# A spectral filter and a two-layer network on one core: the first batch's stages reordered and its last one regrouped, the second batch's first stage split between two engines

## The chip, the cores and the metric

One core of one Trainium2 chip. In the profiles PE is the tensor engine (matmuls), PEld its weight loads, DVE the vector engine, ACT the scalar engine and POOL (Pool) GpSimd; PSUM is the memory that matmuls write to, and a cast here is a copy out of it to 16 bits. The granted clock is the share of its full clock that PE was given. The metric is the device time of one execution in microseconds. Each kernel is run several times. Before: 793.71 us median of 6 runs (792.79 to 795.1).

## The reference

`x` is (8, 3008, 256). Each batch is filtered along its 3008 positions in the frequency domain, and the result goes through a leaky two-layer network.

```python
X = np.fft.rfft(x, axis=1)
Y = X * (filt_r + 1j * filt_i)[None]
y = np.fft.irfft(Y, n=3008, axis=1)          # (8, 3008, 256)
h = y.reshape(24064, 256) @ w_in             # 256 -> 2048
out = np.maximum(0.01 * h, h) @ w_out        # 2048 -> 256, float32
```

## The kernel before

The transform is split as 3008 = 94 x 32. Per batch: stage 1 (`s1`, 94-point matmuls), a transpose on DVE (`t1`), stage 2 and the filter (`s2`, DVE and Pool multiply), the inverse of stage 2 (`sa`), a second transpose (`t2`) and the last stage (`sb`), which leaves `yts`, columns by token. Then PE runs the network in 47 chunks of 512 tokens with 8 slots each. The first batch runs alone, because nothing dense can start before it is done; the other batches are strewn over the slots by `plan`.

```python
def s1_group(b, g):                    # 2 matmuls, then one cast PSUM -> SBUF on ACT
    ...
    spread(big[(4 * b) % 3], 2 * g, ps, nc.scalar.copy)

def spread(dst, n0, ps, copy, e0=0):   # column d goes to pair e = d // 2, place t = d % 2
    copy(paired(dst)[:, ds(n0, nn), ds(e0, de)], ps[:].rearrange("p n (e t) -> p n e t", t=2))

def t2_part(b, i):                     # 32 x 32 transposes of pairs seen as 4-byte words
    a = big[(4*b+2) % 3]...            # read in order e, n
    o = big[(4*b+3) % 3]...rearrange("p (h n e) -> p h e n", h=2, n=Q)
    nc.vector.transpose(o[:, i // 2, ts(i % 2, E4), :], a)     # one word, then 256 bytes on

def sb_group(b, g, copy, pool=(pfp, "pf")):
    for j in range(4):
        nc.tensor.matmul(ps[:, j, :], src[:, dt, 4 * h + j, :], i1_sb[:, 4 * h + j, :], ...)
    copy(yv[:, :, ds(4 * h, 4)], ps[:].rearrange("p c a -> p a c"))
...
# the first batch, in halves of 128 columns; True: Pool multiplies (ACT brings it the PSUM), False: DVE
upper(0)
first_s2(0, 0, 8, False)
first_s2(0, 8, 8, True)
first_s2(0, 16, 4, False)
first_s2(0, 20, 4, True)
for g in range(8): first_s1(1, g, ...)
t1_part(0, 2, True)(), t1_part(0, 3, True)()
first_sa(0, 0), first_sa(0, 16)
upper(1)                               # 2.75 us of ACT and 0.95 of DVE: filter rows copied
first_s2(1, 0, 8, False)
first_s2(1, 8, 8, True)
first_sa(0, 8), first_sa(0, 20)
first_s2(1, 16, 8, False)
first_sa(1, 0)
t2_part(0, 0)(), t2_part(0, 1)()
first_sa(1, 16), first_sa(1, 8)
t2_part(0, 2)(), t2_part(0, 3)()
keep_warm(5)                           # 5 matmuls whose result nobody reads
...                                    # sb_group 0 to 7
keep_warm(3)
...                                    # sb_group 8 to 15
plan(1, 0, 0, 3, 6, 10, 4, 3, 25, 31)  # batch 1: s1 from slot 0, t1 slot 6, s2 slot 10, t2 25, sb 31
```

Pool's products go to a pool of four buffers shared with the output tiles (`outp.tile([P, n, DH], FP16, tag="ost")`); each `first_s2(..., True)` takes two of them.

Of the kernel before, what the change touches and what calls it, by code (L numbers as in the profile page):

```python
# [10 lines left out]
P = 128  # L11
FP16 = mybir.dt.float16
FP32 = mybir.dt.float32
# [5 lines left out]
N1, N2 = 94, 32  # L19
NC = 24  # L20
Q = 32
# [44 lines left out]
def kernel(  # L66
# [9 lines left out]
    nc = tc.nc  # L76
# [18 lines left out]
    i1_sb = cpool.tile([P, N2, N1], FP16, name="i1_sb")  # L95
# [6 lines left out]
    big = [cpool.tile([P, Q * D], FP16, name=f"big{i}") for i in range(3)]  # L102
    yts = [cpool.tile([P, NDT, N], FP16, name=f"yt{i}") for i in range(2)]
# [16 lines left out]
    DH = D // 2  # L120

    def x_load(b, n0=0, nn=N2, d0=0, dn=D):

        for lo, cnt in ((0, R1),) if b + 1 < B else ((0, 64), (64, N1 - 64)):
            nc.gpsimd.dma_start(  # L125
                x_sb[lo : lo + cnt, ds(n0, nn), ds(d0, dn)],
                bass.AP(tensor=x.tensor, offset=x.offset + (b * N + lo * N2 + n0) * D + d0,
                        ap=[[N2 * D, cnt], [D, nn], [1, dn]]))
# [10 lines left out]
    step = N2 // FP  # L139
# [15 lines left out]
    nc.vector.memset(big[2][:].rearrange("p (e n t) -> p e n t", n=Q, t=2)[:, :, NC:Q, :], 0.0)  # L155


    def s1_group(b, g):
        def go():
            ps = pfp.tile([P, 2, D], FP32, tag="pf", name=f"s1_b{b}_g{g}")  # L160
            for j in range(2):
                n2 = 2 * g + j
                nc.tensor.matmul(ps[:, j, :], f1_sb[:N1, n2, :], x_sb[:N1, n2, :],  # L163
                                 start=True, stop=True)
            spread(big[(4 * b) % 3], 2 * g, ps, nc.scalar.copy)
        return go


    def paired(t):
        return t[:].rearrange("p (e n t) -> p n e t", n=Q, t=2)  # L170

    def spread(dst, n0, ps, copy, e0=0):
        nn, de = ps.shape[1], ps.shape[2] // 2
        copy(paired(dst)[:, ds(n0, nn), ds(e0, de)], ps[:].rearrange("p n (e t) -> p n e t", t=2))  # L174

    E4 = D // 2 // 4

    def t1_part(b, i, flat=False):
        def go():
            a = big[(4 * b) % 3][:].bitcast(FP32)[:, ts(i, E4 * Q)].rearrange("p (e n) -> p e n", n=Q)  # L180
            o = big[(4 * b + 1) % 3][:].bitcast(FP32)
            if flat:
                o = o[:, ts(i, E4 * Q)].rearrange("p (e n) -> p e n", n=Q)
            else:
                o = o.rearrange("p (n e) -> p e n", n=Q)[:, ts(i, E4), :]
            nc.vector.transpose(o, a)  # L186
        return go


    def t2_part(b, i):  # L190
        def go():
            a = big[(4 * b + 2) % 3][:].bitcast(FP32)[:, ts(i, E4 * Q)].rearrange("p (e n) -> p e n", n=Q)
            o = big[(4 * b + 3) % 3][:].bitcast(FP32).rearrange("p (h n e) -> p h e n", h=2, n=Q)
            nc.vector.transpose(o[:, i // 2, ts(i % 2, E4), :], a)  # L194
        return go
# [19 lines left out]
    def sa_group(b, g):  # L215
        def go():
            ps = pfp.tile([P, 2, D], FP32, tag="pf", name=f"sa_b{b}_g{g}")
            nc.tensor.matmul(ps[:], inv2, ys.pop((b, g))[:], start=True, stop=True)  # L218
            spread(big[(4 * b + 2) % 3], 2 * g, ps, nc.scalar.copy)
        return go  # L220

    def sb_group(b, g, copy, pool=(pfp, "pf")):
        dt, h = g // 8, g % 8

        def go():
            src = big[(4 * b + 3) % 3][:].rearrange("p (h n d) -> p h n d", h=2, n=Q)
            ps = pool[0].tile([P, 4, N1], FP32, tag=pool[1], name=f"sb_b{b}_g{g}")
            for j in range(4):
                n2 = 4 * h + j
                nc.tensor.matmul(ps[:, j, :], src[:, dt, n2, :], i1_sb[:, n2, :],  # L230
                                 start=True, stop=True)
            yv = yts[b % 2][:, dt, :].rearrange("p (a c) -> p a c", c=N2)
            copy(yv[:, :, ds(4 * h, 4)], ps[:].rearrange("p c a -> p a c"))  # L233
        return go


    two = ((pfp, "pf"), (php, "ph"))
    act, dve = nc.scalar.copy, nc.vector.tensor_copy
# [10 lines left out]
    def first_s2(hf, c, n, on_pool):  # L249
        ps = php.tile([P, n, DH], FP32, tag="ph", name=f"f2_h{hf}_c{c}")  # L250
        src = paired(big[1])
        for j in range(0, n, 4):
            nc.tensor.matmul(ps[:, ds(j, 4), :].rearrange("p n (e t) -> p n e t", t=2), fwd2,  # L253
                             src[:, ds(c + j, 4), ts(hf, DH // 2)], start=True, stop=True)
        fs = [f[:, ds(c, n), ts(hf, DH)] for f in (fa_sb, fb_sb)]
        if on_pool:
            y = [outp.tile([P, n, DH], FP16, tag="ost", name=f"fy{i}_h{hf}_c{c}") for i in range(2)]
            xs = [scrp.tile([P, 4, DH], FP32, tag=f"p{j // 4 + 1}", name=f"fx_h{hf}_c{c + j}")
                  for j in range(0, n, 4)]
            for j, xf in enumerate(xs):  # L260
                act(xf[:], ps[:, ts(j, 4), :])
            for i in range(2):
                for j, xf in enumerate(xs):
                    nc.gpsimd.tensor_tensor(y[i][:, ts(j, 4), :], xf[:], fs[i][:, ts(j, 4), :], AL.mult)
        else:
            y = [ypp.tile([P, n, DH], FP16, tag=f"yw{i}", bufs=2, name=f"fy{i}_h{hf}_c{c}")
                 for i in range(2)]
            for i in range(2):
                nc.vector.tensor_tensor(y[i][:], ps[:], fs[i], AL.mult)  # L269
        ys[(hf, c)] = y  # L270

    def first_sa(hf, c):
        y = ys.pop((hf, c))
        for j in range(0, y[0].shape[1], 4):
            ps = pfp.tile([P, 4, DH], FP32, tag="pf", name=f"fa_h{hf}_c{c + j}")
            for i, m in enumerate((inv2, inv2x)):
                nc.tensor.matmul(ps[:], m, y[i][:, ds(j, 4), :], start=(i == 0), stop=(i == 1))
            spread(big[2], c + j, ps, act, hf * DH // 2)

    def upper(hf):  # L280
        for t, cp in ((fa_sb, act), (fb_sb, dve)):
            cp(t[64:P, :, ts(hf, DH)], t[0:64, :, ts(hf, DH)])


    def keep_warm(n):
        for _ in range(n):
            nc.tensor.matmul(po_ps[:].rearrange("p a d -> p (a d)"), small_sb[:, 0, :],
                             i1_sb[:].rearrange("p a d -> p (a d)")[:, 0:512],
                             start=True, stop=True)
# [2 lines left out]
        first_s1(0, g, two[(g // 2) % 2], (act, dve)[g % 2])  # L292
    t1_part(0, 0, True)(), t1_part(0, 1, True)()
    upper(0)
    first_s2(0, 0, 8, False)
    first_s2(0, 8, 8, True)
    first_s2(0, 16, 4, False)
    first_s2(0, 20, 4, True)
    for g in range(8):
        first_s1(1, g, two[0], dve if g in (1, 3, 6) else act)  # L300
    x_load(1)
    t1_part(0, 2, True)(), t1_part(0, 3, True)()
    first_sa(0, 0), first_sa(0, 16)
    upper(1)
    first_s2(1, 0, 8, False)
    first_s2(1, 8, 8, True)
    nc.gpsimd.dma_start(w_out_sb[:], moe_w_out.rearrange("(ct p) d -> p ct d", p=P))
    first_sa(0, 8), first_sa(0, 20)
    first_s2(1, 16, 8, False)
    first_sa(1, 0)  # L310
    t2_part(0, 0)(), t2_part(0, 1)()
    first_sa(1, 16), first_sa(1, 8)
    t2_part(0, 2)(), t2_part(0, 3)()
    keep_warm(5)
    for g in range(8):
        sb_group(0, g, act, two[(g // 2) % 2])()
    keep_warm(3)
    for g in range(8, 16):
        sb_group(0, g, (act, dve)[g % 2], two[(g // 2) % 2])()

    nc.gpsimd.tensor_scalar(fb_sb[64:P], fb_sb[64:P], -1.0, None, AL.mult)

# [47 lines left out]
    def at(slot, f):  # L370
        tasks.setdefault(slot, []).append(f)

    def plan(b, s1, first, per, t1, s2, step, lag, t2, sb):
        for i, g in enumerate(range(first, 16)):
            at(s1 + i // per, s1_group(b, g))
        if b + 1 < B:
            at(s1 + (15 - first) // per, lambda: x_load(b + 1))
        for i in range(4):
            at(t1 + i, t1_part(b, i))
            at(t2 + i, t2_part(b, i))  # L380
        for g in range(12):
            at(s2 + (step * g) // 4, s2_group(b, g))
            at(s2 + lag + (step * g) // 4, sa_group(b, g))
        for g in range(16):
            at(sb + g // 2, sb_group(b, g, nc.vector.tensor_copy))

    plan(1, 0, 0, 3, 6, 10, 4, 3, 25, 31)
    for b in range(2, B):
        z = 47 * (b - 1) - 8
        plan(b, z, 0, 2, z + 9, z + 13, 5, 3, z + 32, z + 37)  # L390

    for slot in range(SL * (NCHUNK + 1)):
        ci, g = divmod(slot, SL)
# [36 lines left out]
```

## Time and profile before

| | before |
|---|---|
| median of 6 runs | 793.71 us |
| span of the profiled run | 790.6 us |
| PE busy | 761.7 us (96%) |
| first dense matmul (M) | 44.73 us |
| second batch's first stage-2 matmul (S) | 66.78 us |

Besides the lines that the prediction shows, one view of the kernel before is of use later: PE in order of time (start, length, engine, line, operation, output and inputs, shapes, count, and in brackets the idle time before and what ended it), at the last stage of the first batch.

```profile
38.98 1.24 PE L230 MATMUL sb_b_g<-i_sb,big 128*128 128x94 f16 x24 [0.93 <-DVE big L194]
40.64 0.71 PE L230 MATMUL sb_b_g<-i_sb,big 128*128 128x94 f16 x8 [0.42 <-ACT yt L233]
...
42.55 1.95 PE L230 MATMUL sb_b_g<-i_sb,big 128*128 128x94 f16 x32 [0.56 <-DVE big L194]
```

The 64 full matmuls of that stage wait for the second pair of transposes (0.56 us ahead of 42.55), and then 32 of them take 1.95 us.

### The profile page before, as it was taken

The numbers are of one execution on the slowest core, as the hardware profiler recorded it, in microseconds if no ns is written. First come the engines' busy times: TensorE is split into PE (matmuls) and PEld (weight loads), VectorE is DVE, ScalarE is ACT, GpSimd is POOL, SyncE is SP. The second block draws the span as 40 slices with busy tenths as digits, with TensorE's granted clock in tenths as the row PEclk, the third lists the DMA queues.
The fourth block names the chain that finished last, engine by engine and source line by source line (L and its number), as shares of the span: only waits on it lengthen the run. The fifth ranks groups of instructions, "written<-read, shape, count | busy, mean of one in ns | idle before, by whom it ended". The sixth has DMA issues, their size and how long they took to land.

```text
span 790.6 us, 13456 instructions
## 1 busy us (share of the span) xinstructions
PE 761.7 (96%) x5748; PEld 526.2 (67%) x5748; DVE 362.5 (46%) x451; ACT 560.3 (71%) x802; POOL 150.6 (19%) x122
## 2 busy tenths in 40 slices
PE   2788999999999999999999999999999999999998
PEld 1345667666776667866678667776677666776666
DVE  4829751675407742376415763077431765200000
ACT  3696768777596766877677776877759776666664
POOL 5863400151002500043000420024000340000000
PEclk9999999999999999999999999999999999999999
DMA  9933101410114010410105010141100101001111
GB/s 175 220 44 86 40 28 41 108 41 27 42 41 107 28 41 28 94 54 34 35 29 119 27 41 34 35 106 41 41 27 28 41 27 41 35 34 41 41 41 54
DMA packets 42011, 43.38 MB, mean 55 GB/s; under 512 B 14274, under 2 KB 40514, under 8 KB 41282
## 3 DMA queue, kind: packets, MB, share of 16 engines
q0 software_dynamic: 15760, 16.99, 13.2%
q1 hardware_dynamic: 26192, 25.53, 9.3%
q8 instruction: 45, 0.74, 0.4%
q14 instruction: 14, 0.11, 0.0%
HBM read 34.10 MB, written 24.64 MB: 74 GB/s over the span
## 4 chain that ended last, share of the span: by engine, by line
PE 92%; ACT 3%; DVE 3%; DMA 1%; issue 0%; POOL 0%; ACTq 0%; DVEq 0%; POOLq 0%
PE po_ps L353 40%; PE h_c_g L339 40%; PE sb_b_g L230 3%; PE s_b_g L163 3%; PE s_b_g L203 2%; PE sa_b_g L218 2%; ACT big L174 2%; DVE big L186 1%; DMA x_sb<-in_x_dram 1%; DVE big L194 1%; PE o_c_t L353 1%; ACT gt_c L344 1%; DVE fy_h_c L269 1%; PE f_h_g L244 1%; PE f_h_c L253 1%
## 5 line engine op out<-in xcount | busy, mean ns | idle before, releaser
L344 ACT ACTIVATE gt_c<-h_c_g 128x1024 f16<-128x1024 f32 x376 | 385.6, 1026 | 196.3 <-PE h_c_g L339 195.3
L339 PE MATMUL h_c_g<-yt,w_in_sb 128*128 128x512 f16 (+7 forms) x1728 | 386.7, 351 | 1.3 <-ACT gt_c L344 1.0
L353 PE MATMUL po_ps<-w_out_sb,gt_c 128*128 128x256 f16 x2944 | 381.4, 272 | 0.5 <-ACT ost_c_t L360 0.5
L353 PEld LDWEIGHTS <-gt_c 128*128 128x128 f16 x3008 | 290.7, 98 | 88.7 <-issue 3.8
L339 PEld LDWEIGHTS <-w_in_sb 128*128 128x128 f16 x1728 | 163.0, 98 | 96.2 <-issue 2.3
L211 POOL TENSOR_TENSOR y_b_g<-p_b_g,p_b_g 128x512 f16<-128x512 f32 x84 | 106.9, 1273 | 225.0 <-DVE p_b_g L209 225.0
L186 DVE STREAM_TRANSPOSE big<-big 128x1024 f32<-128x1024 f32 x32 | 55.7, 1844 | 141.6 <-ACT big L174 141.5
L233 DVE CAST yt<-sb_b_g 128x376 f16<-128x376 f32 x116 | 58.3, 545 | 89.9 <-PE sb_b_g L230 89.9
L207 DVE TENSOR_TENSOR p_b_g<-s_b_g,fa_sb 128x512 f32<-128x512 f32 x84 | 58.1, 692 | 37.3 <-PE s_b_g L203 34.8
L360 ACT COPY ost_c_t<-po_ps 128x256 f32<-128x256 f32 x184 | 69.4, 377 | 7.1 <-PE po_ps L353 5.9
L194 DVE STREAM_TRANSPOSE big<-big 128x1024 f32<-128x1024 f32 x32 | 58.4, 1940 | 34.2 <-ACT big L174 34.2
L174 ACT CAST big<-s_b_g 128x512 f16<-128x512 f32 x112 | 61.5, 621 | 0.0
L208 DVE TENSOR_TENSOR p_b_g<-s_b_g,fb_sb 64x512 f32<-64x512 f32 x84 | 58.2, 693 | 1.1
L125 POOL DMA_DIRECT2D x_sb<-in_x_dram x12 | 8.5, 713 | 263.0 <-PE s_b_g L163 262.2
L209 DVE TENSOR_TENSOR p_b_g<-s_b_g,fb_sb 64x512 f32<-64x512 f32 x84 | 57.4, 684 | 1.1
L174 ACT CAST big<-sa_b_g 128x512 f16<-128x512 f32 x84 | 50.6, 602 | 0.0
L230 PEld LDWEIGHTS <-big 128*128 128x128 f16 x512 | 28.7, 98 | 16.6 <-DVE big L194 2.5
L163 PE MATMUL s_b_g<-x_sb,f_sb 94*128 94x256 f16 x224 | 34.6, 272 | 1.6 <-ACT big L174 0.7
L230 PE MATMUL sb_b_g<-i_sb,big 128*128 128x94 f16 x512 | 32.5, 206 | 2.0 <-DVE big L194 1.5
L203 PE MATMUL s_b_g<-big,small_sb 128*128 128x512 f16 x84 | 31.8, 379 | 1.8 <-DVE big L186 1.8
L218 PE MATMUL sa_b_g<-y_b_g,small_sb 128*128 128x512 f16 x84 | 31.8, 379 | 0.0
L163 PEld LDWEIGHTS <-f_sb 94*128 94x128 f16 x224 | 20.9, 97 | 12.2 <-issue 4.4
(37 smaller groups left out, 135.5 us busy)
## 6 DMA issues: line engine op xcount, KB each, us to landing
out_dram<-ost_c_t SPq DMA_DIRECT2D x92, 256.0 KB, 2.1
x_sb<-in_x_dram POOLq DMA_DIRECT2D x6, 1536.0 KB, 10.8
x_sb<-in_x_dram POOLq DMA_DIRECT2D x4, 384.0 KB, 10.4
w_in_sb<-in_moe_w_in_dram POOLq DMA_DIRECT2D x1, 1024.0 KB, 15.3
w_out_sb<-in_moe_w_out_dram POOLq DMA_DIRECT2D x1, 1024.0 KB, 10.7
x_sb<-in_x_dram POOLq DMA_DIRECT2D x1, 1024.0 KB, 8.0
f_sb<-fwd_const SPq DMA_DIRECT2D x4, 192.0 KB, 3.5
fa_sb<-in_filt_r_dram POOLq DMA_DIRECT2D x4, 192.0 KB, 10.0
```

Of the source, the lines that this page charges most:

```text
L163: nc.tensor.matmul(ps[:, j, :], f1_sb[:N1, n2, :], x_sb[:N1, n2, :], start=True, stop=True)
L174: copy(paired(dst)[:, ds(n0, nn), ds(e0, de)], ps[:].rearrange("p n (e t) -> p n e t", t=2))
L186: nc.vector.transpose(o, a)
L194: nc.vector.transpose(o[:, i // 2, ts(i % 2, E4), :], a)
L208: nc.vector.tensor_tensor(p2[0:64], ps[64:P], fb[64:P], AL.mult)
L211: nc.gpsimd.tensor_tensor(y1[:], p1[:], p2[:], AL.add)
L230: nc.tensor.matmul(ps[:, j, :], src[:, dt, n2, :], i1_sb[:, n2, :], start=True, stop=True)
L233: copy(yv[:, :, ds(4 * h, 4)], ps[:].rearrange("p c a -> p a c"))
L339: nc.tensor.matmul(ph[:, j, ds(o, ln)], w_in_sb[:, dt, ts(ct, P)], yts[b % 2][:, dt, ds(lo, ln)], start=(dt == 0), stop=(dt == NDT - 1),)
L344: nc.scalar.activation(gts[ci][:, ds(2 * g, 2), :], ph[:], AF.Lrelu)
L353: nc.tensor.matmul(po, gts[ci][:, ct, ts(tj, P)], w_out_sb[:, ct, :], start=(ct == 0), stop=(ct == NCT - 1))
L360: nc.scalar.copy(ost[:, tj % 2, :], po)
```

## The change

Its intent: (A) take half of the second batch's first-stage casts from ACT, which bounds that stage, and let its second stage start two slots later, so that PE no longer waits for its transpose; (B) in the first batch, give Pool its group first and copy the filter rows earlier; (C) let the second transpose write two neighbouring words (8 bytes) by pairing column d with d + 64 and ordering the words `(n e r)`; (D) since a column of the operand is then met only every 8 bytes, run the last stage in two 64-column halves, 128 matmuls instead of 64.

```diff
--- before.py
+++ after.py
@@ -155,14 +155,14 @@
     nc.vector.memset(big[2][:].rearrange("p (e n t) -> p e n t", n=Q, t=2)[:, :, NC:Q, :], 0.0)
 
 
-    def s1_group(b, g):
+    def s1_group(b, g, copy=nc.scalar.copy):
         def go():
             ps = pfp.tile([P, 2, D], FP32, tag="pf", name=f"s1_b{b}_g{g}")
             for j in range(2):
                 n2 = 2 * g + j
                 nc.tensor.matmul(ps[:, j, :], f1_sb[:N1, n2, :], x_sb[:N1, n2, :],
                                  start=True, stop=True)
-            spread(big[(4 * b) % 3], 2 * g, ps, nc.scalar.copy)
+            spread(big[(4 * b) % 3], 2 * g, ps, copy)
         return go
 
 
@@ -275,7 +275,26 @@
             ps = pfp.tile([P, 4, DH], FP32, tag="pf", name=f"fa_h{hf}_c{c + j}")
             for i, m in enumerate((inv2, inv2x)):
                 nc.tensor.matmul(ps[:], m, y[i][:, ds(j, 4), :], start=(i == 0), stop=(i == 1))
-            spread(big[2], c + j, ps, act, hf * DH // 2)
+            act(paired(big[2])[:, ds(c + j, 4), ts(hf, DH // 2)],
+                ps[:].rearrange("p n (t e) -> p n e t", t=2))
+
+
+    def first_t2(i):
+        a = big[2][:].bitcast(FP32)[:, ts(i, E4 * Q)].rearrange("p (e n r) -> p e n r", n=Q // 2, r=2)
+        o = big[0][:].bitcast(FP32).rearrange("p (h n e r) -> p h e n r", h=2, n=Q // 2, r=2)
+        nc.vector.transpose(o[:, i // 2, ts(i % 2, E4)], a)
+
+    def first_sb(g, copy, pool):
+        dt, h = g // 8, g % 8
+        src = big[0][:].rearrange("p (h n e r t) -> p h n r t e", h=2, n=Q // 2, r=2, t=2)
+        ps = pool[0].tile([P, 4, N1], FP32, tag=pool[1], name=f"fb_g{g}")
+        for j in range(4):
+            n2 = 4 * h + j
+            for t in range(2):
+                nc.tensor.matmul(ps[64 * t : 64 * t + 64, j, :], src[:, dt, n2 // 2, n2 % 2, t, :],
+                                 i1_sb[:, n2, :], start=True, stop=True)
+        yv = yts[0][:, dt, :].rearrange("p (a c) -> p a c", c=N2)
+        copy(yv[:, :, ds(4 * h, 4)], ps[:].rearrange("p c a -> p a c"))
 
     def upper(hf):
         for t, cp in ((fa_sb, act), (fb_sb, dve)):
@@ -292,31 +311,31 @@
         first_s1(0, g, two[(g // 2) % 2], (act, dve)[g % 2])
     t1_part(0, 0, True)(), t1_part(0, 1, True)()
     upper(0)
+    first_s2(0, 8, 8, True)
     first_s2(0, 0, 8, False)
-    first_s2(0, 8, 8, True)
+    first_s2(0, 20, 4, True)
     first_s2(0, 16, 4, False)
-    first_s2(0, 20, 4, True)
     for g in range(8):
         first_s1(1, g, two[0], dve if g in (1, 3, 6) else act)
     x_load(1)
     t1_part(0, 2, True)(), t1_part(0, 3, True)()
+    upper(1)
     first_sa(0, 0), first_sa(0, 16)
-    upper(1)
-    first_s2(1, 0, 8, False)
     first_s2(1, 8, 8, True)
     nc.gpsimd.dma_start(w_out_sb[:], moe_w_out.rearrange("(ct p) d -> p ct d", p=P))
+    first_s2(1, 0, 8, False)
+    first_s2(1, 16, 8, False)
     first_sa(0, 8), first_sa(0, 20)
-    first_s2(1, 16, 8, False)
     first_sa(1, 0)
-    t2_part(0, 0)(), t2_part(0, 1)()
+    first_t2(0), first_t2(1)
     first_sa(1, 16), first_sa(1, 8)
-    t2_part(0, 2)(), t2_part(0, 3)()
+    first_t2(2), first_t2(3)
     keep_warm(5)
     for g in range(8):
-        sb_group(0, g, act, two[(g // 2) % 2])()
+        first_sb(g, act, two[(g // 2) % 2])
     keep_warm(3)
     for g in range(8, 16):
-        sb_group(0, g, (act, dve)[g % 2], two[(g // 2) % 2])()
+        first_sb(g, (act, dve)[g % 2], two[(g // 2) % 2])
 
     nc.gpsimd.tensor_scalar(fb_sb[64:P], fb_sb[64:P], -1.0, None, AL.mult)
 
@@ -370,24 +389,25 @@
     def at(slot, f):
         tasks.setdefault(slot, []).append(f)
 
-    def plan(b, s1, first, per, t1, s2, step, lag, t2, sb):
-        for i, g in enumerate(range(first, 16)):
-            at(s1 + i // per, s1_group(b, g))
+    def plan(b, s1, per, t1, s2, step, lag, t2, sb):
+        for g in range(16):
+            at(s1 + g // per, s1_group(b, g, dve if b == 1 and g % 2 else act))
         if b + 1 < B:
-            at(s1 + (15 - first) // per, lambda: x_load(b + 1))
+            at(s1 + 15 // per, lambda: x_load(b + 1))
         for i in range(4):
             at(t1 + i, t1_part(b, i))
-            at(t2 + i, t2_part(b, i))
         for g in range(12):
             at(s2 + (step * g) // 4, s2_group(b, g))
             at(s2 + lag + (step * g) // 4, sa_group(b, g))
+        for i in range(4):
+            at(t2 + i, t2_part(b, i))
         for g in range(16):
-            at(sb + g // 2, sb_group(b, g, nc.vector.tensor_copy))
-
-    plan(1, 0, 0, 3, 6, 10, 4, 3, 25, 31)
+            at(sb + g // 2, sb_group(b, g, dve))
+
+    plan(1, 0, 3, 6, 12, 4, 3, 26, 31)
     for b in range(2, B):
         z = 47 * (b - 1) - 8
-        plan(b, z, 0, 2, z + 9, z + 13, 5, 3, z + 32, z + 37)
+        plan(b, z, 2, z + 9, z + 13, 5, 3, z + 32, z + 37)
 
     for slot in range(SL * (NCHUNK + 1)):
         ci, g = divmod(slot, SL)
```

A variant that gives both halves as one 128-column operand, which would have spared the doubled count, does not build: the builder wants a stationary operand "with exactly one free dimension". So D comes with C.

## The prediction

> **What bounds the kernel now.** I first read the page's busy line, then busy time by stretches, to see where PE has room. The columns are PE, weight loads, DVE, ACT, POOL, then PE clock, DMA share and GB/s.
>
> ```profile
> PE 761.7 (96%) x5748; PEld 526.2 (67%) x5748; DVE 362.5 (46%) x451; ACT 560.3 (71%) x802; POOL 150.6 (19%) x122
> ```
>
> ```profile
> 10.00:36.00 26.00, 16.91 (x92) 8.82 (x91) 20.89 (x22) 17.79 (x25) 16.81 (x19) 1.00 1.46 217
> 36.00:45.00 9.00, 6.78 (x78) 4.13 (x77) 8.38 (x8) 6.67 (x16) 9.00 (x1) 1.00 0.95 127
> 45.00:67.00 22.00, 17.42 (x94) 8.91 (x93) 7.32 (x5) 18.66 (x28) 7.17 (x2) 1.00 0.37 73
> ...
> 100.00:400.00 300.00, 299.82 (x2334) 209.89 (x2332) 154.66 (x198) 217.68 (x311) 47.38 (x39) 1.00 0.18 50
> ```
>
> From 67 us to 778 us PE is never idle. This steady state is untouched by the change, so only the first 67 us can give anything: whatever PE idles less there comes off the end one for one. The chain that ended last, in order of time (start, length, what), shows what holds that start:
>
> ```profile
> 24.98 0.89 ACT big L174 x2
> 25.87 0.10 issue
> 25.97 0.63 ACT big L174
> 26.60 0.02 issue
> 26.62 2.76 ACT fa_sb L282
> 29.38 0.02 issue
> 29.41 2.37 DVE fy_h_c L269 x2
> ...
> 32.88 2.36 DVE fy_h_c L269 x2
> 35.23 7.28 DVE big L194 x4
> ...
> 42.55 1.24 PE sb_b_g L230 x24
> ...
> 44.73 0.38 PE h_c_g L339
> ...
> 48.50 0.92 ACT gt_c L344
> 49.41 1.47 ACT big L174 x3
> ...
> 59.49 7.24 DVE big L186 x4
> 66.73 0.04 issue
> 66.78 0.38 PE s_b_g L203
> 67.15 0.87 PE po_ps L353 x8
> ```
>
> The reader sees two parts. Until 44.73 the first batch's transform runs with the second DVE transpose (7.28 us) on the path; 44.73 is the first dense matmul (I call it M). From 45.99 to 59.47 ACT is the bound: each slot is one activation (0.92) and three casts of the second batch's first stage (1.47), 2.39 us, while PE needs about 0.86 + 6 x 0.11 = 1.5. Then the second batch's first transpose (7.24) holds PE, in its waits for 1.8 us:
>
> ```profile
> PE s_b_g L203 <- DVE big L186: 1.8, 1, 1.8
> ```
>
> **What the Trainium skill says.** (1) "SBUF — State Buffer", Specifications (TRN2), gives 16-byte lines that need at least two hits per line for full bandwidth. The trace agrees in kind. Two first-stage transposes, which write contiguously, take 2.37 us; four second ones, which write single 4-byte words 256 bytes apart, take 7.35, so 1.19 against 1.84 each for the same elements.
>
> ```profile
> 24.92 2.37 DVE L186 STREAM_TRANSPOSE big<-big 128x1024 f32<-128x1024 f32 x2 [0.32 <-ACT big L174]
> 35.15 7.35 DVE L194 STREAM_TRANSPOSE big<-big 128x1024 f32<-128x1024 f32 x4
> ```
>
> (2) "TensorEngine Tiling (Array Packing)", Restrictions: column tiling switches the fast weight load off; its Key Properties say that changing the mode drains the array and that tiles can load and multiply in parallel. (3) "TensorE: Matmul & The Clock Gate", LDWEIGHTS: a weight load takes columns / 1.2 ns, so 53 ns for 64 columns as an estimate from that page. Before has no column tiling, so its trace can't confirm (2) and (3).
>
> **The change part by part.**
>
> *A, second batch, first stage.* ACT casts all 16 groups now; afterwards DVE takes the 8 odd ones. Also the second stage starts in slot 12 instead of 10. ACT for eight slots becomes 8 x 0.93 + 8 x 0.49 = 11.4 us instead of 8 x 0.93 + 16 x 0.49 = 15.3. Eight DVE casts at 0.69 (the mean of its casts in the first batch) lie beside that: 1.0 us in a slot of 1.7. Walking the slots by hand with three buffers for the first stage and two for the dense results, ACT stays the bound: first activation at M + 1.26 (as before, 45.99 - 44.73), last cast on DVE at about M + 10.3, the ninth dense group finished at about M + 12.6, against 61.30 - 44.73 = 16.6 before: 4.0 us gained. The four strided transposes of 1.81 now end at M + 10.3 + 7.2 = M + 17.5. The PE stream reaches slot 12's second stage at M + 12.6 + 4 x 1.735 = M + 19.5, so the transpose wait (1.84 in the chain) goes too. Check by PE work: before, 11 dense groups (0.865), 32 first-stage matmuls (0.109) and two slices (0.87) are 14.8 us of 22.05, so idle 7.3; after, 9 groups and the 32 matmuls are 11.3 of 12.6, idle 1.3. Gain 6.0 us.
>
> *B, order in the first batch's first three stages.* Pool's group first: its multiply starts about 0.9 earlier (18.5 instead of 19.4), but DVE's groups come one PE pair later (18.73 instead of 17.96), its three casts with them, and the second half's transpose starts at about 25.35 instead of 24.92. The big weight copy (2.76, ACT) moves ahead of three casts, to 25.3 to 28.05, and no longer gates DVE, which instead waits for PE's second pair: at half 1 the four matmuls took 1.88 from 27.34, now about 27.8 to 29.65. DVE starts at 29.7 instead of 29.41; the last multiply ends at about 35.5 instead of 35.23. Pool's second group ends near 34.7, as before. But the first half's other three groups now stand behind the last DVE-dependent matmul on PE, so nine ACT casts of 0.54 run from about 33.5 to 38.4; the last ended at 37.87 before. Loss about 0.3 to 0.5 us.
>
> *C, transpose in 8-byte runs.* Each new line now gets two words, so I take the contiguous rate: 1.2 us each instead of 1.84. The first pair runs 35.5 to 37.9; the second waits for ACT's last cast and runs 38.4 to 40.9. Before it ended at 42.51, so 1.6 us earlier. ACT's read of PSUM now steps between halves, but the copies of the last stage also read PSUM with a step and still take 0.39 us for 376 elements; I expect 0.5 to 0.54 per cast as before.
>
> *D, last stage in halves.* 64 matmuls become 128, with 128 weight loads of 64 columns. Before, a pair of load and matmul goes at 0.35 / 8 = 43.6 ns once PE streams:
>
> ```profile
> 108.59 0.35 PE sb_b_g L230 x8
> ```
>
> I take 50 ns per half, between the streaming time and the 53 ns estimate of a slow load: 64 x 50 = 3.2 us per half of the stage, where 32 full ones would be 1.4 and the copies (8 x 0.39 on ACT) set 3.1. PE would start at 38.35 behind its five warming matmuls, finish the first half at 41.55, do three more warming matmuls (0.65) and the second half at 42.2 to 45.4, with the last DVE copy (0.55) the dense stage starts at M = 46.0. So the transposes, ready at 40.9, are no longer the bound: PE is, and M moves from 44.73 by +1.3.
>
> Sum: 793.4 - 6.0 (A) + 1.3 (B, C and D together) = 788.7 us.
>
> **The rivals.** R1: the two column halves overlap, at 25 ns per half. Then copies and transposes bind, the second half ends near 43.3, M moves by -1.3 and the time is about 786. For it: the tiling page's parallel tiles; against it: two instructions per matmul in 43.6 ns is the fastest issue this trace shows. R2: the halves serialise with their loads, 53 + 42 = 95 ns per half. Each half-stage takes 6.1 us, M goes to 51.9 (+7), and the time is about 794.5: the gain of A is eaten. For it: slow loads that don't hide; against it: in before a 98 ns load record is entirely hidden at 43.6 ns per pair. R3: 8-byte runs don't speed the transpose (1.84 stays). PE hides most of it; M loses about 0.8 more, time about 789.5. R4: in A the wait comes back, because DVE's casts are held up by ACT's buffers and its transposes start later than M + 12.3; two microseconds of slack cover it, so I see at most 1 us in it.
>
> **Range and chances.** The central walk is 788.7; R1 gives the low side, R2 the high side. Range 785.5 to 792.0. Two per cent is 15.9 us, more than the whole idle time that can be had (7.3 in the dense start plus a few before M), so faster by 2% has 1%; a loss of 15.9 would need more than R2, 1%; within 2% is 98%.
>
> **What would show it.** In the stretch of M to M + 20, PE idle falls from 7.3 to about 1.3, the wait for the first transpose is gone, and DVE has eight casts there. The second transposes take about 1.2 us each. The half matmuls come at 50 ns in a stream and the chain before M runs through PE's last stage instead of a 7.28 us transpose. If M comes later than 49 or earlier than 43.5, step D is wrong; if the ninth dense group ends later than M + 14, step A is.

## The result, and the profile after

The changed kernel takes 788.38 us median (787.95 to 789.06, 6 runs), before 793.71. The ratio is 0.9932, with a 95% interval from 0.9919 to 0.9945. A ratio here is the mean time of one kernel's fast runs over the mean of the other's in the same rounds, so not quite the ratio of the medians. The predicted 788.7 and its range hold the result. The steps did not all hold.

The chain that ended last, changed kernel (start, length, what):

```profile
32.09 1.05 PE f_h_c L253 x2
...
33.16 2.37 DVE fy_h_c L269 x2
...
35.68 3.40 POOL fy_h_c L264 x3
...
39.12 0.38 PE fa_h_c L277
39.49 1.08 PE po_ps L306 x5
40.57 0.40 PE fb_g L294 x8
...
42.27 0.82 PE fb_g L294 x16
43.09 0.75 PE po_ps L306 x3
43.84 1.88 PE fb_g L294 x55
...
46.27 0.38 PE h_c_g L358
...
48.44 1.12 ACT big L174 x2
49.56 0.90 ACT gt_c L363
...
57.22 1.94 PE h_c_g L358 x8
...
66.10 0.22 PE s_b_g L203
```

Against the chain of before, the reader sees three things. The 7.28 us of DVE transposes are gone from it, as the prediction said. In their place stand PE's last stage (with 128 half matmuls) and, ahead of it, 3.40 us of Pool, which the prediction did not forecast. And after M (46.27) the wait for the second batch's transpose is gone: one slot of ACT is 0.90 plus one or two casts instead of three, the ninth dense group ends at 59.16, and PE runs without a break into S (here one step of the chain at 66.10, in the order of PE 65.94).

DVE and Pool of the changed kernel in order of time:

```profile
36.07 2.37 DVE L285 STREAM_TRANSPOSE big<-big 128x1024 f32<-128x1024 f32 x2 [0.55 <-ACT big L278]
40.16 2.38 DVE L285 STREAM_TRANSPOSE big<-big 128x1024 f32<-128x1024 f32 x2 [1.72 <-ACT big L278]
```

```profile
34.55 2.28 POOL L264 TENSOR_TENSOR fy_h_c<-fx_h_c,fa_sb 128x512 f16<-128x512 f32 x2 [8.95 <-issue]
36.80 2.27 POOL L264 TENSOR_TENSOR fy_h_c<-fx_h_c,fb_sb 128x512 f16<-128x512 f32 x2
```

The first of the two Pool lines, in the kernel before:

```profile
30.07 2.27 POOL L264 TENSOR_TENSOR fy_h_c<-fx_h_c,fa_sb 128x512 f16<-128x512 f32 x2 [3.37 <-ACT fx_h_c L261]
```

And PE of the changed kernel just before its last stage:

```profile
32.09 1.03 PE L253 MATMUL f_h_c<-big,small_sb 128*128 128x512 f16 x2 [2.51 <-DVE fy_h_c L269]
32.94 4.57 PE L277 MATMUL fa_h_c<-fy_h_c,small_sb 128*128 128x512 f16 x15
```

Two transposes now take 2.37 us, that is 1.2 each, the same as the contiguous ones. But the second pair starts at 40.16 where I had 38.4, and it waited 1.72 us for a cast of ACT, which in turn waited for the matmul that reads Pool's product. Pool's second group started at 34.55, after 8.95 us with "issue" as the reason, that is, nothing the profile names; before it started at 30.07.

The page's busy time and the stretch around M:

```profile
PE 763.3 (97%) x5812; PEld 527.9 (67%) x5812; DVE 365.0 (46%) x459; ACT 556.9 (71%) x794; POOL 150.6 (19%) x122
```

```profile
45.00:67.00 22.00, 21.08 (x156) 13.14 (x153) 14.97 (x17) 18.14 (x26) 11.66 (x2) 1.00 0.53 98
```

PE is busy 21.08 of the 22 us where it was 17.42 before; over the whole span its busy time is nearly the same.

**Four marks for all experiments.** I read four times from PE and DVE in order of time: X, the second block of stage-1 matmuls (it starts when the second part of the first input lands, which differs by over 2 us from one profiled run to the next); Y, the end of the last DVE multiply of the first batch; M, the first dense matmul; S, the second batch's first stage-2 matmul. Differences between marks are free of the input's luck. PE's work from M to S is 14.8 us where S stands in slot 10 (11 dense groups, 32 stage-1 matmuls, 2 slices, as in the prediction), and 18.2 where it stands in slot 12 (13 x 0.865 + 32 x 0.109 + 4 x 0.87); S - M less that is PE's idle time. (A stretch from M to S in the views shows less of it, 4.6 us in before and 0.7 in the changed kernel, because there each matmul counts as busy up to its modelled end.)

| kernel | median us | ratio to before (95%) | X to Y | Y to M | M to S | idle M to S |
|---|---|---|---|---|---|---|
| before | 793.71 | 1 | 23.65 | 9.49 | 22.05 | 7.3 |
| changed | 788.38 | 0.9932 (0.9919 to 0.9945) | 24.18 | 10.74 | 19.67 | 1.5 |
| e1, A alone | 787.24 | 0.9924 (0.9912 to 0.9936) | 24.72 | 9.49 | 19.73 | 1.5 |
| e2, B C D alone | 794.56 | 1.0008 (0.9994 to 1.0022) | 24.16 | 10.75 | 22.05 | 7.3 |
| e8, slots alone | 791.76 | 0.9976 (0.9963 to 0.9988) | 24.22 | 9.49 | 23.54 | 5.3 |
| e9, changed less B | 786.07 | 0.9914 (0.9900 to 0.9927) | 23.62 | 8.50 | 19.70 | 1.5 |
| e3, own buffers for Pool | 787.04 | 0.9926 (0.9914 to 0.9939) | 24.17 | 9.61 | 19.72 | 1.5 |
| e4, inverse groups earlier | 785.67 | 0.9909 (0.9896 to 0.9923) | 24.16 | 8.50 | 19.72 | 1.5 |
| e5, 4-byte words | 788.54 | 0.9945 (0.9932 to 0.9957) | 24.16 | 10.78 | 19.68 | 1.5 |
| e6, one half at a time | 789.16 | 0.9951 (0.9937 to 0.9964) | 24.14 | 10.82 | 19.71 | 1.5 |
| e10, e9 with 4-byte words | 788.35 | 0.9938 (0.9924 to 0.9952) | 24.72 | 9.63 | 19.72 | 1.5 |
| e12, e4 without warmers | 785.91 | 0.9902 (0.9888 to 0.9916) | 24.17 | 8.20 | 20.01 | 1.8 |
| e14, e4 with early warmers | 786.62 | 0.9913 (0.9897 to 0.9929) | 24.08 | 8.51 | 19.70 | 1.5 |

The marks come from one profiled run each, so the time interval of about 1 us and the marks support each other: the marks show a mechanism to a tenth, the times only that it is real in sum. The experiments were timed in four groups (e1, e2, e8, e9; e3 to e6; e10, e12, e13; e14), each of the first three with its own runs of before (e14 was compared with those of e10's group and one more), so ratios of different groups are compared with care. e4, e12 and e14 have 4 timed runs, the others 5, the changed kernel 6.

### The profile page after: what moved, and what is told of

It is laid out like the page before. It is cut to its first block, busy times and chain, and to the rows that moved or that the text cites. A ratio compares the mean times of both kernels' runs of the same rounds, so it can differ in the third digit from the quotient of the medians.

```text
span 786.4 us, 13584 instructions
## 1 busy us (share of the span) xinstructions
PE 763.3 (97%) x5812; PEld 527.9 (67%) x5812; DVE 365.0 (46%) x459; ACT 556.9 (71%) x794; POOL 150.6 (19%) x122
## 4 chain that ended last, share of the span: by engine, by line
PE 93%; ACT 3%; DVE 2%; DMA 1%; POOL 1%; issue 1%; POOLq 0%; ACTq 0%; DVEq 0%
PE po_ps L372 41%; PE h_c_g L358 40%; PE s_b_g L163 3%; PE sb_b_g L230 2%; PE s_b_g L203 2%; PE sa_b_g L218 2%; DMA x_sb<-in_x_dram 1%; DVE fy_h_c L269 1%; PE o_c_t L372 1%; ACT big L174 1%; ACT gt_c L363 1%; PE f_h_g L244 0%; POOL fy_h_c L264 0%; PE fb_g L294 0%; ACT fa_sb L301 0%
## 5 line engine op out<-in xcount | busy, mean ns | idle before, releaser
L186 DVE STREAM_TRANSPOSE big<-big 128x1024 f32<-128x1024 f32 x32 | 55.8, 1843 | 127.3 <-ACT big L174 127.1
L233 DVE CAST yt<-sb_b_g 128x376 f16<-128x376 f32 x112 | 56.3, 545 | 85.9 <-PE sb_b_g L230 85.9
L194 DVE STREAM_TRANSPOSE big<-big 128x1024 f32<-128x1024 f32 x28 | 51.1, 1933 | 34.5 <-ACT big L174 34.5
L174 ACT CAST big<-s_b_g 128x512 f16<-128x512 f32 x104 | 57.0, 607 | 0.0
L230 PEld LDWEIGHTS <-big 128*128 128x128 f16 x448 | 25.6, 98 | 13.2
L230 PE MATMUL sb_b_g<-i_sb,big 128*128 128x94 f16 x448 | 28.7, 206 | 0.0
```

Of the source, the lines that this page charges most:

```text
L230: nc.tensor.matmul(ps[:, j, :], src[:, dt, n2, :], i1_sb[:, n2, :], start=True, stop=True)
```

## The experiments

My theory after the result: A is the whole gain, and the first batch's part (B, C, D together) costs about 1.5 us; the cost is B, by Pool's late second group, and not D. Rivals: D's doubled matmuls cost; or C's faster transposes are what gains.

**e1: A alone.** The kernel before with the changed `s1_group` and `plan`.

```diff
-    plan(1, 0, 0, 3, 6, 10, 4, 3, 25, 31)
+    plan(1, 0, 3, 6, 12, 4, 3, 26, 31)      # and: copy = dve if b == 1 and g % 2 else act
```

> Step A alone (casts shared with DVE, second stage from slot 12), first batch as in the kernel before. Theory (A is the whole gain, 5.7 us): the first dense matmul stays at about 44.5 to 44.7 us, the wait of 1.8 us for the first transpose is gone, ninth dense group at M + 12.6 to 12.9, time about 788.0 against 793.7. Rival (the first-batch part is what gains): time near 792, and the stage M to M + 20 still holds over 4 us of PE idle time.

787.24 us. The chain from M on has the form of the changed kernel's; the wait for the transpose is gone, and the eighth and ninth dense groups run together at 56.64:

```profile
45.63 0.38 PE h_c_g L339
...
56.64 1.94 PE h_c_g L339 x8
```

so the ninth group ends at 58.58, M + 12.95, and PE's idle time falls from 7.3 to 1.5. The theory holds: A alone gives the full gain, 0.9924 (6.0 us of 793.5). M came at 45.63, later than in before although the first batch is unchanged; see "the half rate" below.

**e2: B, C and D alone.** The changed kernel with the old `plan` and `s1_group`.

> Steps B, C and D alone, second batch planned as in the kernel before. Theory (this part costs): the first dense matmul comes at 46.0 to 46.5, 1.3 to 1.8 later, and the time is about 795.2. Rival (faster transposes gain): first dense matmul before 44.5 and time near 793.

794.56 us, 1.0008 with an interval across 1, so in time it can't be told from no change; the marks show M 1.25 us later after Y than in before, and X to Y within what the order of before itself shows. (M itself came at 47.44, not 46.0 to 46.5, in a run whose input landed 0.94 us later than in before.) The old wait is there again:

```profile
69.49 0.38 PE L203 MATMUL s_b_g<-big,small_sb 128*128 128x512 f16 x1 [1.83 <-DVE big L186]
```

The rival (these parts gain) is out; of the theory, 1.25 us in the marks is shown and 1.5 in the time is not.

**e8: the slots alone.** Before, with stage 2 in slot 12 and the last transposes in 26.

> The kernel before with the second stage moved from slot 10 to 12 and nothing else. Theory: the 1.8 us wait for the first transpose goes and the ACT-bound casts stay, so about 791.9 (1.8 less). Rival: the slots alone give most of step A, under 790; or nothing, 793.7, if the delay comes back later as a wait for the last transposes.

791.76 us, 0.9976, that is 1.9 us less. (The last transposes moved by one slot as well, so the expectation's "nothing else" is not quite so.) The two parts of A are the slots (idle 7.3 to 5.3) and the shared casts (5.3 to 1.5).

**e9: the changed kernel without B.** A, C and D with the first batch's order of before.

```diff
+    first_s2(0, 0, 8, False)
     first_s2(0, 8, 8, True)
-    first_s2(0, 0, 8, False)
...
+    first_sa(0, 0), first_sa(0, 16)
     upper(1)
-    first_sa(0, 0), first_sa(0, 16)
...                                  # and first_sa(0, 8), first_sa(0, 20) before first_s2(1, 16, 8)
```

> The changed kernel with the order of the kernel before in the first batch (step B undone; A, C and D kept). Theory (B costs 1.5 to 2.2 us, by Pool's second group that started at 34.6 instead of 30.1, behind PE's release of its output buffers): Pool's second group starts at about 30, PE's last stage at about 38.1 instead of 40.5, first dense matmul at about 44.1 instead of 46.3, time about 786.3. Rival (D's doubled matmuls cost, as the prediction said): first dense matmul at 45.5 or later, time 788 or more.

786.07 us, faster than the changed kernel. PE in order of time:

```profile
39.11 2.58 PE L294 MATMUL fb_g<-i_sb,big 128*64 128x94 f16 x64
...
42.38 2.27 PE L294 MATMUL fb_g<-i_sb,big 128*64 128x94 f16 x64
44.88 1.21 PE L358 MATMUL h_c_g<-yt,w_in_sb 128*128 128x512 f16 x4 [0.24 <-ACT yt L297]
```

From Y (36.38) to the last stage it is 2.7 us, where it is 5.0 in the changed kernel (35.53 to 40.50). The stage itself takes the same 2.58 and 2.27. So the cost sits before the last stage, in B, and it is 2.24 us in the marks (10.74 to 8.50); the ratios, 0.9932 and 0.9914, put it at 1.4 us with intervals that overlap slightly. Pool's second group starts at 31.21 here; it and M come about 1 us later than expected, since the input landed 1.4 us later than in the changed kernel.

**e3: buffers of its own for Pool's second group.**

```diff
-  y = [outp.tile([P, n, DH], FP16, tag="ost", ...
+  y = [outp.tile([P, n, DH], FP16, tag="ost" if hf == 0 else f"fy{i}", bufs=4 if hf == 0 else 1, ...
```

> The changed kernel, with output buffers of their own for Pool's group of the second half, so that it need not wait for PE to read the first half's. From the landing of the second part of the first input (second block of first-stage matmuls) to the first dense matmul it is 34.92 us in the changed kernel and 33.1 to 34.2 in three kernels with the first batch of before. Theory (the buffer is Pool's wait): Pool's second group starts at about 30.2 instead of 34.6 when the input lands as in the changed kernel, the two waits of PE for Pool (1.0 us) are gone, and that distance falls to 33.5 to 34.0, time about 787.3. Rival (PE's order, not the buffer, sets the end): Pool starts earlier, but the distance stays within 0.3 of 34.9.

Pool no longer waits for "issue", it waits for its input:

```profile
29.47 2.26 POOL L265 TENSOR_TENSOR fy_h_c<-fx_h_c,fa_sb 128x512 f16<-128x512 f32 x2 [4.60 <-ACT fx_h_c L262]
```

Input and Pool are both earlier here (X is 0.7 earlier than in the changed kernel), so Pool's start moved by 4.4 us against X. X to M is 33.78, in the band of the theory. The unnamed wait is thus shown: the two products of the second half went to buffers that PE had yet to read. That is 1.13 of the 2.24 us. The other 1.11 are still there with the buffers free: ACT casts without a break from 34.15 to 38.52, and PE runs five inverse matmuls at half rate (one every 427 ns instead of 215, 1.06 us in all).

**e4: the first half's other inverse groups back in front of the last stage-2 group.** Pool still goes first.

```diff
     first_s2(1, 0, 8, False)
-    first_s2(1, 16, 8, False)
     first_sa(0, 8), first_sa(0, 20)
+    first_s2(1, 16, 8, False)
```

> The changed kernel, with the three inverse groups of the first half put back in front of the last second-stage group on PE (Pool's group still first, weight copy still early). Theory (those groups standing behind a matmul that waits for DVE is what delays both Pool's buffers and ACT's casts): Pool's second group starts at about 30.2, PE does not fall to its slow rate after 32 us, and the distance from input to first dense matmul falls from 34.9 to about 33.0 to 33.3, time about 786.5. Rival (Pool's group first is itself the loss): the distance stays above 34.2.

785.67 us; all of the 2.24 us is back by this one line. Two things come with it. PE frees Pool's buffers at about 30, so the wait of e3 is gone too. And PE does not stand idle from 29.6 to 32.1. Busy time by stretches (PE, weight loads, DVE, ACT, POOL, then PE clock, DMA, GB/s), changed kernel first, then e4:

```profile
30.00:32.00 2.00, 0.00 (x0) 0.00 (x0) 2.00 (x2) 0.60 (x2) 0.00 (x0) 0.89 0.94 201
32.00:34.00 2.00, 1.91 (x5) 0.70 (x6) 0.87 (x2) 0.00 (x0) 0.00 (x0) 0.50 0.96 205
34.00:36.00 2.00, 2.00 (x8) 0.79 (x7) 1.52 (x2) 1.73 (x4) 1.45 (x2) 0.76 1.18 254
```

```profile
30.00:32.00 2.00, 0.91 (x5) 0.20 (x2) 2.00 (x2) 2.00 (x5) 1.59 (x2) 1.00 0.98 209
32.00:34.00 2.00, 1.88 (x6) 0.53 (x6) 0.88 (x2) 0.51 (x2) 2.00 (x3) 1.00 0.88 188
34.00:36.00 2.00, 0.81 (x4) 0.30 (x4) 2.00 (x3) 0.72 (x2) 2.00 (x2) 1.00 1.23 262
```

In the changed kernel PE does nothing from 30 to 32, and its granted clock is then 0.50 in the next stretch, just where the inverse groups stand in a row behind the late matmul; in e4 the clock stays at 1.00. So e4 takes away three things at once, Pool's wait, the casts that came late on ACT and the half clock; e3 parts the first from the other two, and no run parts those. The page "TensorE: Matmul & The Clock Gate" of the Trainium skill describes this: an idle PE falls to half of its clock and needs a while of work to come back (The HAM clock gate). The trace agrees in kind (the clock fell to 0.50 and came back); its times are in the last section. The rival (Pool's group first is itself the loss) is out: e4 keeps it and has the same 8.50 from Y to M as e9.

**e5: 4-byte words in the changed kernel.** Pairing and halves stay.

```diff
-        o = ...rearrange("p (h n e r) -> p h e n r", h=2, n=Q // 2, r=2)
+        o = ...rearrange("p (h n r e) -> p h e n r", h=2, n=Q // 2, r=2)
```

> The changed kernel with its second transpose writing single 4-byte words again, everything else (pairing with d + 64, halves) as it is. Theory (the transposes have slack behind Pool and PE here): each transpose takes about 1.84 us instead of 1.2, the first pair still ends before PE's last stage starts, and the first dense matmul moves by 0.1 to 0.3 us only, time within 0.5 of the changed kernel. Rival (faster transposes are on the path): the first dense matmul comes 0.8 us or more later.

788.54 us, and Y to M is 10.78 against 10.74. The transposes are slow again:

```profile
35.77 7.81 DVE L285 STREAM_TRANSPOSE big<-big 128x1024 f32<-128x1024 f32 x4 [0.68 <-ACT big L278]
```

That is 1.95 us each, short waits included, and the end doesn't move. So in the kernel as changed, C gains nothing: what B made late hides it.

**e10: the same, where Pool is not late** (e9 with 4-byte words).

> The kernel e9 (order of before, A, C and D) with single 4-byte words in the second transpose: C undone, D kept. From the last DVE multiply's end to the first dense matmul it is 9.5 us in before and in e1 and e8 (4-byte words, full columns), 8.5 in e9. Theory (with Pool's wait gone the transposes are on the path and C is worth 1.0; the halves, D, cost next to nothing): 9.4 to 9.6, and time about 787.1. Rival (D costs and C pays for it): over 9.8.

DVE in order of time:

```profile
35.60 7.42 DVE L285 STREAM_TRANSPOSE big<-big 128x1024 f32<-128x1024 f32 x4
```

Y to M is 9.63 against 8.50 in e9: the four transposes follow Y (35.68) without a break and end at 43.02. So with B out of the way C is worth 1.1 us. The granted clock fell to 0.50 from 33.3 to 36.6 in this profile and not in e9's, but the unbroken transposes cover that. The median is 788.35, 2.3 us above e9's (by the ratios 1.9), more than the 1.1. In the two profiled runs X to Y was 24.72 here and 23.62 there; whether that also parted the other runs is not shown. D can be read off as well: e10 and e1 differ in the halves and in the pairing, and from Y to M they take 9.63 and 9.49, so D costs 0.14 where slow transposes hold up PE's last stage. What it costs behind fast ones no run shows, since C doesn't build without it.

**e6: one half at a time.** In the last stage, the four matmuls of one half and then the four of the other.

```diff
-        for j in range(4):
-            n2 = 4 * h + j
-            for t in range(2):
+        for t in range(2):
+            for j in range(4):
+                n2 = 4 * h + j
```

> The changed kernel with the four matmuls of one 64-column half issued before the four of the other, instead of alternating. Theory (the two halves overlap in the array, which is why a half comes every 21 ns in a stream, half of the 43.6 of a full matmul): without alternation a half takes about 42 ns, the second half-stage 2.7 us or more instead of 2.26, first dense matmul 0.5 to 0.9 later. Rival (a half is simply short, whatever stands next to it): 24 halves in 0.5 us as before, no change.

No change (Y to M 10.82; 55 matmuls in 1.91 us of the chain instead of 1.88). The number in my expectation was misread: a stretch counts every instruction that touches it, so 24 matmuls of 0.238 us in a stretch of 0.5 are one every (0.5 + 0.238) / 24 = 31 ns (estimate from these counts), not 21, and 16 full ones of 0.205 one every 44 ns. The experiment decides little, since four of one half and four of the other both lie in PE's queue.

**e13: one half of the array alone.** All half matmuls write the lower 64 rows; the result is wrong on purpose (relative error 0.37). The copies read these rows alone, and the upper ones are cleared once.

```diff
-    nc.tensor.matmul(ps[64 * t : 64 * t + 64, j, :], src[:, dt, n2 // 2, n2 % 2, t, :],
+    nc.tensor.matmul(ps[0 : 64, j, :], src[:, dt, n2 // 2, n2 % 2, t, :],
```

> The changed kernel with every half matmul written to the lower 64 output rows, one half after the other, so that no two can lie in different columns of the array (wrong result on purpose: the upper rows of the transform are zero). Theory (halves overlap only with the other column half, the order of e6 leaving enough of both in the queue): with one half alone the rate falls from 24 to about 12 in 0.5 us (42 ns) and the first dense matmul comes about 0.5 to 1 us later. Rival (a half matmul costs 21 ns wherever it stands): 24 in 0.5 us.

```profile
41.93 3.99 PE fb_g L296 x64
...
46.68 4.01 PE fb_g L296 x64
```

64 half matmuls take 4.0 us, one every 62.5 ns, exactly twice the 31 ns of the changed kernel. So two halves overlap when they write different halves of the rows and do not when they write the same; one alone costs more than a full matmul (43.6). The edit changes the array's columns and the output rows together, so which of the two stands in the way is not shown. In the sense of the expectation the theory holds with other numbers: the rate halves. Whether the 62.5 ns are the weight load or the load and the product one after the other, no run tells. The time of this one run (793.02) is not compared, since one run has no interval and its state is unknown.

**e12: e4 without the eight warming matmuls.**

```diff
-    keep_warm(5)
-    keep_warm(3)
```

> The kernel e4 without the eight warming matmuls before and within PE's last stage. Theory (PE's order, warmers included, is what now sets the first dense matmul): from the last DVE multiply's end to the first dense matmul 7.6 to 8.0 instead of 8.49, time about 785.0. Rival (without them PE loses its fast clock, or ACT's copies bind): 8.3 or more and time 785.7 or above.

785.91 us, no better than e4. Its chain:

```profile
40.84 2.28 PE fb_g L294 x57
43.12 0.56 issue
43.69 0.40 PE fb_g L294 x6
...
44.10 0.56 DVE yt L297
...
44.71 0.82 PE h_c_g L356 x3
```

PE now waits 0.56 us ("issue": the profile names no reason; that it is a PSUM buffer which a copy has yet to free is likely and not shown) and the last copy (DVE, 44.10) ends as late as before. The first dense matmul starts at 44.00 on the half that is ready, and the next ones wait until 44.71, so that Y to S is 28.21 us against 28.22 in e4. In its size the result lies between the theory (up to 8.0 from Y to M) and the rival (8.3 or more): 8.20. By the time and the chain the rival's second half was right, the copies bind; its first half was not, the granted clock stays at 1.00 from 28.46 on.

**e14: e4 with seven matmuls in PE's wait for the first transpose.** They run from 13.26 to 16.45, themselves at half rate (one every 427 ns).

> The kernel e4 with seven matmuls of 512 columns while PE waits for the first transpose (13 to 16.5 us). Theory (PE multiplies at half rate for its first inverse groups, six matmuls in 2.72 us instead of 1.46, because it idled shortly before; kept busy it stays fast): the second first-stage half and those six run faster, and from the landing of the input's second part to the last DVE multiply it is 23.0 to 23.7 us instead of 24.17, time about 785.0. Rival (those matmuls lie beside ACT's weight copy and the casts, off the path, or the rate has another cause): 24.1 to 24.2 again, time as e4, 785.7.

786.62 us, and the six inverse matmuls still take 2.62 us; X to Y is 24.08. The theory falls. See the next paragraph.

**The half rate.** The five kernels with the order of before share their code up to Y, and X to Y came out as 23.65, 24.72, 24.22, 23.62 and 24.72. Six matmuls of the first half, in before and in e1:

```profile
24.35 1.46 PE L277 MATMUL fa_h_c<-fy_h_c,small_sb 128*128 128x512 f16 x6
```

```profile
24.15 2.72 PE L277 MATMUL fa_h_c<-fy_h_c,small_sb 128*128 128x512 f16 x6
```

With 2.72 us they hold up ACT's weight copy, and all behind it by 1.1; with the copy ahead of them (the kernels with B's early copy) they are slow as well in every profile, 2.62 to 2.72 us, but X to Y stays between 24.08 and 24.18 there (e13, with an extra clearing of memory, is left out). The stretches show a granted clock of 1.00 there in both, but only because the trace's clock record has no entry that early. Its first entry, the full clock, begins at 23.27 us in before and 24.53 in e9, whose six matmuls are fast; at 26.47 in e8, where the change falls within the fourth of them:

```profile
25.05 2.14 PE L277 MATMUL fa_h_c<-fy_h_c,small_sb 128*128 128x512 f16 x6
```

and at 27.89 in e1 and 26.46 in e10, where all six are slow. The starts of the matmuls agree: in before, stage-1 matmuls start every 107 ns up to about 23.3 and every 55 after that; in e8 the gaps within the six are 379, 426, 427, 313 and 217 ns. So PE runs at half rate from its first matmul on, and what differs between executions is when the full clock begins. In the order of before that was 11.7 to 16.5 us after X, in the nine profiles with B's order 15.5 to 17.8. Why it begins when it does is not shown: in e14 PE was busy from 11.60 to 18.63 but for one gap of 0.28 us, and the full clock still came only at 27.08, so idling just before the first transpose is not the only cause.

## Why the prediction was right, and where it was right by luck

**A (predicted -6.0).** Right in size and by its steps. The first activation is at M + 1.25 (1.26 predicted), the last DVE cast ends at 56.67, M + 10.4 (10.3), the ninth dense group at M + 12.9 (12.6), the transposes at 64.06, M + 17.8 (17.5), and S at M + 19.7 (19.5). Idle time fell from 7.3 to 1.5 (1.3); e1 measures 6.0.

**B (predicted a loss of 0.3 to 0.5).** The step failed in size: 2.24 us by e9 and e4. X to Y was right (24.18 against 23.65 in before; over the five profiles of the old order the mean is 24.19, so no loss is shown there. The 23.65 had the early full clock; against the 24.72 of a late one B's early weight copy gains 0.5, because it no longer waits for the slow matmuls). What the walk lacked is in its line "Pool's second group ends near 34.7, as before": Pool ended at 39.07. I had written down that three groups now stand behind the last DVE-dependent matmul on PE, and counted only ACT's casts behind them. But the same groups read Pool's buffers, and Pool needed those for its next product (e3: 1.13 us). The other 1.11 us are the casts that come late on ACT, which the prediction had seen (33.5 to 38.4), and the half clock after PE's gap of 2.50 us, which it had not; how they divide is not shown, since e4 undoes both.

**C (predicted 1.6 earlier, hidden behind PE).** 1.2 us per transpose is right. That it does not show is right as well, but what hides it is what B made late, Pool's group first, and not PE's last stage; uncovered it is worth 1.1 (e10).

**D (predicted 50 ns per half, 3.2 us per half-stage).** Too much: 31 ns in the stream, and 2.59 and 2.26 us with the copies. Rival R1 (overlap) was the right mechanism at 31 instead of 25 ns; that weight loads do not hide (R2, 95, in which 42 ns for the product came without a source) is refuted. D costs 0.14 us behind slow transposes. R3 and R4 did not come: the transposes take 1.2 us, and in A they are done at 64.06, 1.9 us before S needs them.

So of the +1.3 for B, C and D, B was about 1.8 too small and D about 1.55 too large (0.6 and 0.95 in its two half-stages), and the two errors cancelled: M was predicted at 46.0 and came at 46.27, or 46.5 on the input's clock of before. The signs that the prediction had set for a wrong D (M before 43.5 or after 49) could not catch this. The total of -4.7 against the measured -5.3 owes its closeness to that, and only A's part of it to understanding.

**A better version.** e4, the changed kernel with one line moved, takes 785.67 us (0.9909); e9 (0.9914) and e12 (0.9902) can't be told from it.

## What to carry to other kernels

When an engine's instructions are reordered, ask of each one that moves back not only who reads its result but whose buffers it frees: the wait it makes can appear on an engine that the change doesn't touch, as a long "issue" with no name. A gap on PE can be paid twice, since the clock may drop in it; whether it does is not read off its length alone (2.16 us dropped it in e10, 2.15 did not in e1). A total that comes out as predicted proves the total only; undo the parts one by one before believing the terms. A view that prints a clock of 1.00 may only lack a record: check it by how far apart equal matmuls start (here 427 ns or 215). And take the noise between executions of the same code (here 1.1 us before Y) as the smallest term that can be read off a single trace.

## What the Trainium skill lacked or had wrong

- "TensorE: Matmul & The Clock Gate", advises in its table for kernels no PE gaps over about 3 us ("Why this matters for your kernels"). Shorter ones can do it. Here PE ended a matmul at 29.59 and started the next at 32.09, a gap of 2.50 us; by the trace's clock record the full clock ended at 31.55, 2.0 us into the gap, and came back at 34.96, 2.9 us after PE resumed (stretches within these times show 1.00, 0.50 and 1.00). In e10 a gap of 2.16 us brought 0.50 from 33.3 to 36.6, in e1 one of 2.15 us left 1.00.
- "TensorEngine Tiling (Array Packing)" gives up to 2 times the speed for two 64-column tiles and says that they switch the fast weight load off, but not what that leaves at a small moving size. Here, with 94 moving columns: a full matmul every 43.6 ns, a pair of halves every 62 ns (31 each), one half alone every 62.5 ns. Against one half alone the pair has the page's factor of 2 (31 ns to 62.5). Against the full matmul that it replaces it is a loss of 1.4 times on PE, so splitting a full 128 columns gains nothing here.
- "SBUF — State Buffer", Specifications (TRN2), has the two hits per line; I found no page that gives what a DVE transpose pays for missing it. Here 1.19 us contiguous, 1.84 in single words, 1.2 in pairs of words.
- I found no page that says that a wait for a buffer that another engine has yet to read can appear with no releaser; here it was 8.95 us of Pool put down to "issue", and e3 showed the buffer.
